# A four-token layout for the first 512 tokens, and a new split of the first loads over two DMA queues

## The chip, the cores and the metric

One core of one Trainium2 chip. The metric is the device time of one execution in microseconds, the median of several; the "span" of a profile is a little shorter (95.0 us in a run of 96.57). Runs are marked fast or slow; for one core, slow means over 1.5% above the fastest of the same kernel.

## The reference, cut to what matters

An mLSTM cell (4 batches, 8 heads, 768 tokens, head size 40) and behind it a maxout MLP.

```python
for t in range(S):
    m_new  = np.maximum(f_gate[:, :, t] + m, i_gate[:, :, t])
    f_stab = np.exp(f_gate[:, :, t] + m - m_new); i_stab = np.exp(i_gate[:, :, t] - m_new); m = m_new
    C = f_stab * C + i_stab * outer(v_t, k_t);  n = f_stab * n + i_stab * k_t      # shapes left out
    y[:, :, t] = sigmoid(o_gate_t) * (C @ q_t) / max(|n . q_t|, 1)
x = y.transpose(0, 2, 1, 3).reshape(B * S, H * D)      # 3072 x 320
out = maximum(x @ w1, x @ w2) @ w_out                  # 320 -> 1024 -> 320
```

The kernel uses that, with these gates, only the first 42 tokens add to the state to working accuracy. It checks this at run time and has a general path for other data, which never runs here.

## The kernel before: the parts that the change touches

SP, A, V, G are the queues or engines of SyncE, ScalarE, VectorE and GpSimd. `load_seg(g, ...)` loads tokens of batch 0: with `c1-c0` chunks, partition p holds that many neighbouring tokens, so one contiguous run is 160 bytes per chunk.

```python
SEG = ((0, 1), (1, 4), (4, 6))            # chunks of 128 tokens of batch 0 that are loaded together
...
SP.dma_start(out=f_sb[:, 0:L], in_=fv[:, 0:L])        # small: 16 KB
A.dma_start(out=i_sb[:, 0:L], in_=iv[:, 0:L])         # small: 16 KB
load_kv(0, 1, k, kst, SP)                             # small: 336 runs of 160 bytes
load_kv(0, 1, v, vst, A)
load_seg(0, q, qst, "qst", SP)                        # 1024 runs of 160 bytes
load_seg(0, o_gate, ost, "ost", A)
load_seg(1, q, qst, "qst", SP)                        # 1024 runs of 480 bytes
load_seg(1, o_gate, ost, "ost", SP)
load_w(0, 0, SP)                                      # then the weights, wo, later pieces: all SP
...
def idle(n):                                          # dummy matmuls, 512 columns each
    ...
idle(8)
# gates: F = cumsum(f); a = i - F; running maximum; Exp; transposed to gT   (V, A, TensorE)
# vw = v * gT on V; kT, vb (values), cq (the state) from TensorE through V
...
def f_h(n, pool=None, eng=V, dup=V):                  # chunk c of batch b
    first = c == 0                                    # first chunk: masked scores P; others: the state
    for s in range(NS):
        lhsT, rhs = (Pm[b][m, s, :], vb[b][m]) if first else (qT[b][rows(s), c, s, :], cq[b][rows(s)])
        nc.tensor.matmul(ph[...], lhsT, rhs[...], start=True, stop=True)
    ...                                               # y = (gate + 1) * ph          on V
    if n % 2:
        cp(dup)(out=y[:, DM:DM + 64], in_=y[:, 2 * DM:2 * DM + 64])    # a 64-column duplicate
...
f_h(1, pp_o, V, A); f_h(2, None); f_h(3, pp_o, V, A)  # duplicates on ScalarE
idle(3)
w_diff(0, 0, G); w_diffx(G); w_cast(0, 0, A)          # w1 - w2, and bf16 of w2
f_y(0, A, pp_o); idle(3); f_y(2, V)                   # transposes of y
g = up(0, 0, True)                                    # first MLP matmuls
...
```

`PLAN`, a table of two dozen lines, says which small operation of the later batches is issued beside which group of MLP matmuls.

## Time and profile before

| | before |
|---|---|
| median time | 96.83 us (96.66 to 97.06) |
| first MLP matmul | 13.54 us |
| from there to the last matmul's start | 78.1 us |
| from there to the end | 3.3 us |

After the first MLP matmul, TensorE has hardly a gap; so the time is the start of that stretch plus its length plus the tail.

### The profile page before, as it was taken

Reading aid. Unit: us, or ns where it says so; the run is one execution under the profiler, and the core shown is the slowest. Engines: PE = TensorE matmul, PEld = TensorE weight load, DVE = VectorE, ACT = ScalarE, POOL = GpSimd, SP = SyncE. Lnnn points to the kernel's source line nnn. Section 1 sums busy time; section 2 is a strip of 40 time slices with the busy share of each in tenths; the row PEclk is TensorE's granted clock in tenths of the full one; section 3 lists DMA queues with packets and bytes.
Section 4 is the critical chain, followed back from the end, with each engine's and each line's share of the span. In section 5 each row is a group of like instructions: output and inputs, shape, how many; then the busy total and the mean of one; then the engine's idle time right before and its main releaser. Section 6 shows DMA issues by size and latency. Waiting matters only on the chain.

```text
span 95.0 us, 2293 instructions
## 1 busy us (share of the span) xinstructions
PE 88.6 (93%) x884; PEld 65.3 (69%) x885; DVE 57.3 (60%) x167; ACT 42.0 (44%) x59; POOL 27.9 (29%) x67
## 2 busy tenths in 40 slices
PE   2998969999999999999999999999999999999960
PEld 1345547777788878688777868777686767877650
DVE  4997836953778999988843438649640442123240
ACT  0895784683241771391809068070713425070000
POOL 5146398763747070912271000002500000000000
PEclk9999999999999999999999999999999999999999
DMA  0999999997999989998969978393532030303052
GB/s 14 171 270 331 387 388 372 355 256 124 284 294 269 175 207 368 312 166 155 310 160 268 178 194 214 138 76 69 177 99 72 7 138 10 138 0 133 24 200 65
DMA packets 32701, 17.97 MB, mean 189 GB/s; under 512 B 21808, under 2 KB 30448, under 8 KB 32688
## 3 DMA queue, kind: packets, MB, share of 16 engines
q1 hardware_dynamic: 31250, 17.57, 71.9%
q10 hardware_dynamic: 1438, 0.23, 1.5%
q8 instruction: 7, 0.11, 0.5%
q14 instruction: 6, 0.05, 0.2%
HBM read 12.42 MB, written 3.93 MB: 172 GB/s over the span
## 4 chain that ended last, share of the span: by engine, by line
PE 79%; DMA 6%; DVE 6%; ACT 3%; SPq 1%; issue 1%; POOL 1%; POOLq 0%
PE po L548 28%; PE pu L479 17%; PE po L544 8%; PE pu L487 6%; DMA qst<-in_q_dram 6%; PE pwc L439 3%; PE pu L453 3%; PE ph L357 3%; PE pq L298 2%; PE py L389 2%; PE po L532 2%; DVE y L367 1%; DVE gt L493 1%; PE pu L460 1%; DVE qT L299 1%
## 5 line engine op out<-in xcount | busy, mean ns | idle before, releaser
L495 ACT ACTIVATE gt<-pu 128x1024 bf16<-128x1024 f32 x18 | 17.6, 1021 | 25.7 <-PE pu L487 24.6
L548 PE MATMUL po<-wo,gt 128*128 128x320 bf16 x160 | 26.9, 299 | 0.0
L479 PE MATMUL pu<-xT,wd 128*128 128x256 bf16 x160 | 20.9, 272 | 0.8 <-ACT xT L390 0.8
L556 DVE COPY o_sb<-po 128x320 f32<-128x320 f32 (+2 forms) x23 | 10.9, 474 | 17.2 <-PE po L548 17.2
L548 PEld LDWEIGHTS <-gt 128*128 128x128 bf16 x160 | 15.0, 98 | 5.2
L479 PEld LDWEIGHTS <-wd 128*128 128x128 bf16 x160 | 15.1, 97 | 3.9 <-issue 1.5
L367 DVE SCALAR_TENSOR_TENSOR y<-ost,ph 128x320 bf16<-128x320 f32 x20 | 9.6, 482 | 3.3 <-PE ph L357 2.2
L544 PE MATMUL po<-Wc_t,xT 128*128 128x320 bf16 (+2 forms) x50 | 10.7, 295 | 0.0
L267 ACT ACTIVATE ost<-ost 128x320 f32<-128x320 f32 (+2 forms) x14 | 8.7, 659 | 3.8 <-DMA ost<-in_o_gate_dram 3.8
L222 PE MATMUL pd<-warm,ident_b 128*128 128x512 bf16 x24 | 7.9, 449 | 1.7 <-POOL ident_b masks.py:199 1.7
L257 POOL CAST qb<-qst 128x240 bf16<-128x240 f32 (+1 forms) x12 | 5.8, 487 | 11.3 <-DMA qst<-in_q_dram 11.3
L487 PE MATMUL pu<-xT,wd 64*128 64x256 bf16 x80 | 6.1, 272 | 0.0
L576 POOL TENSOR_TENSOR a<-i_sb,F 32x640 f32<-32x640 f32 x1 | 1.5, 1528 | 15.5 <-DVE F L574 15.5
L402 POOL TENSOR_TENSOR wd<-w 128x512 bf16<-128x512 f32 x4 | 5.1, 1270 | 2.4 <-DMA w<-in_moe_w_dram 2.3
L544 PEld LDWEIGHTS <-xT 128*128 128x128 bf16 x50 | 4.0, 98 | 2.6 <-issue 1.5
L357 PE MATMUL ph<-cq,qT 120*128 120x123 bf16 (+1 forms) x60 | 5.7, 213 | 0.0
L548 PE MATMUL po<-wo,gs 128*128 128x320 bf16 (+2 forms) x40 | 5.6, 272 | 0.0
L463 ACT ACTIVATE gs<-pu 128x1024 bf16<-128x1024 f32 x4 | 3.9, 1016 | 3.4 <-PE pu L460 3.4
L357 PEld LDWEIGHTS <-qT 120*128 120x128 bf16 (+1 forms) x60 | 4.2, 98 | 1.5 <-ACT qT L299 0.4
L390 DVE COPY xT<-py 128x640 bf16<-128x640 bf16 x7 | 3.4, 492 | 2.7 <-PE py L389 2.5
L222 PEld LDWEIGHTS <-ident_b 128*128 128x128 bf16 x25 | 2.3, 111 | 3.7 <-issue 1.7
L298 PE MATMUL pq<-ident_b,qb 128*128 128x128 bf16 x48 | 4.1, 219 | 0.7 <-POOL qb L262 0.6
(131 smaller groups left out, 124.9 us busy)
## 6 DMA issues: line engine op xcount, KB each, us to landing
qst<-in_q_dram SPq DMA_DIRECT2D x3, 800.0 KB, 5.5
ost<-in_o_gate_dram SPq DMA_DIRECT2D x3, 800.0 KB
out_dram<-o_sb SPq DMA_DIRECT2D x7, 320.0 KB
w<-in_moe_w_dram SPq DMA_DIRECT2D x8, 256.0 KB, 5.4
out_dram<-o_sb SPq DMA_DIRECT2D x9, 160.0 KB, 2.3
wo_st<-in_moe_w_out_dram SPq DMA_DIRECT2D x2, 640.0 KB
qst<-in_q_dram SPq DMA_DIRECT2D x4, 160.0 KB
wx<-in_moe_w_dram SPq DMA_DIRECT2D x2, 256.0 KB
```

The source lines that it names most:

```text
L222: nc.tensor.matmul(pd[:, 0, :], ident_b, warm, start=True, stop=True)
L257: cp(eng)(out=qp[b % 2][:, c0:c1, 0:2, 0:HS3 * D].rearrange("p c s (h d) -> p c s h d", d=D), in_=qst[b][:, 0:6, c0:c1, :].rearrange("p (s ...
L267: A.activation(out=s, in_=s, func=AF.Tanh, scale=0.5)
L298: nc.tensor.transpose(pq[:, j, s, :], qb[b % 2][:, c0:c0 + 128], ident_b)
L357: nc.tensor.matmul(ph[:, vcols(s), :].rearrange("p a b -> p (a b)"), lhsT, rhs[:, vcols(s), :].rearrange("p a b -> p (a b)"), start=True, ...
L367: V.scalar_tensor_tensor(out=yo, in0=ost[b][:, :, c, :], scalar=1.0, in1=ph[:, :, 0:D], op0=OP.add, op1=OP.mult)
L479: nc.tensor.matmul(pus[i][:, j, :], wd[:, c, f * 128:(f + 1) * 128], x[:, :, GA[i][c], :], start=start and j % 2 == 0, stop=stop and j % 2 ...
L487: nc.tensor.matmul(pus[i][:, j, :], wd2[r, f * 128:(f + 1) * 128], x[r, :, 2, :], start=False, stop=stop and j % 2 == 1)
L495: A.activation(out=o, in_=pus[i], func=AF.Relu)
L544: nc.tensor.matmul(po, x[:, s // 2, GA[s % 2][cc], :], Wc_t[:, cc, w], start=False, stop=False)
L548: nc.tensor.matmul(po, gt[:, f, s % 2, s // 2 * L:(s // 2 + 1) * L], wo[:, f, w], start=False, stop=(f == NFF - 1))
L556: cp(eng)(out=o_sb[:, s % 2 if two else 0, :], in_=po)
```

## The change

The intent: hold tokens 4p to 4p+3 in partition p, so that q and o of the first 512 tokens come in 640-byte runs, half as many; start q's load at once by giving it the head of the SyncE queue; and shift weight work and two y transposes out of TensorE's full stretch.

```diff
-    SEG = ((0, 1), (1, 4), (4, 6))
+    SEG = ((0, 4), (4, 6))
+    TC = 11
@@ loads
-    SP.dma_start(out=f_sb[:, 0:L], in_=fv[:, 0:L])
+    load_seg(0, q, qst, "qst", SP)
+    A.dma_start(out=f_sb[:, 0:L], in_=fv[:, 0:L])
     A.dma_start(out=i_sb[:, 0:L], in_=iv[:, 0:L])
-    load_kv(0, 1, k, kst, SP)
+    load_kv(0, 1, k, kst, A)
     load_kv(0, 1, v, vst, A)
-    load_seg(0, q, qst, "qst", SP)
-    load_seg(0, o_gate, ost, "ost", A)
-    load_seg(1, q, qst, "qst", SP)
-    load_seg(1, o_gate, ost, "ost", SP)
+    load_seg(0, o_gate, ost, "ost", SP)
@@ all four chunks take the state; 11 rows of each are then overwritten (cut)
-        first = c == 0
+        first = b > 0 and c == 0
+        if n < 4:
+            yield
+            for s in range(NS):
+                nc.tensor.matmul(ph[0:TC, vcols(s), :]..., Pm[0][m, s, c, :], vb[0][m, vcols(s), :]..., ...)
@@ the mask with the gates in it: three fp32 products (six matmuls in the trace) and one V operation (cut)
+    for s in range(NS):
+        nc.tensor.matmul(pgi[0:KP, s], F[:, L + s * KP:L + s * KP + KP], gr, start=True, stop=True)
+    V.scalar_tensor_tensor(out=mask0[0:KP], in0=tcol0..., scalar=jrow[0:KP], in1=pgi[0:KP], ...)
@@ order (cut)
-    f_h(1, pp_o, V, A)
+    parts = [h_parts(n, (pp_o, pp_f, pp_f, pp_o)[n]) for n in range(4)]     # duplicates now on V
-    f_y(0, A, pp_o)
-    idle(3)
-    f_y(2, V)
+    idle(5)
+    f_y(0, A, pp_u)
+    run(w_trans(0, 0, A, pp_u))
+    f_y(2, V, pp_o)
+    w_fold(0, V, None)
@@ PLAN: every line rewritten; y transposes of pairs 6 and 8 by DMA instead of on TensorE
```

In front of the first MLP matmul stand 18 dummy matmuls instead of 25.

More of the change, by code (lines that the diff above doesn't have):

```diff
@@ L141 @@
     load_wo(1, SP)
-    load_seg(2, q, qst, "qst", SP)
-    load_seg(2, o_gate, ost, "ost", SP)
+    load_seg(1, q, qst, "qst", SP)
+    load_seg(1, o_gate, ost, "ost", SP)
     def load_batch(b, eng):
@@ L179 @@
     tcol = const.tile([128, L], BF, name="tcol")
+    tcol0 = const.tile([128, 4, TC], BF, name="tcol0")
+    ab = const.tile([128, B * NT, H], FP, name="ab")
+    mask0 = ab.rearrange("p n h -> p (n h)")[:, 0:NS * 4 * TC].rearrange("p (s c t) -> p s c t", c=4, t=TC)
     ge = const.tile([128, 2], FP, name="ge")
@@ L195 @@
     V.memset(vw[:, 0], 0.0)
+    G.tensor_copy(out=F[:, L:L + NS * KP].rearrange("p (h j) -> p h j", j=T0),
+                  in_=ident_f[:, 0:H9].unsqueeze(2).to_broadcast([BH, H9, T0]))
     G.memset(sel, 0.0)
     G.memset(vst[:, :, D:D1], 1.0)
-    for c in (1, 4):
+    for c in (4,):
         G.memset(qb[0][:, c * DM:c * DM + 64], 0.0)
+    G.iota(tcol0, pattern=[[1, 4], [4, TC]], base=0, channel_multiplier=0, allow_small_or_imprecise_dtypes=True)
     G.iota(tcol, pattern=[[1, L]], base=0, channel_multiplier=0, allow_small_or_imprecise_dtypes=True)
@@ L234 @@
                   in_=a[:, 0:T0].unsqueeze(1).to_broadcast([BH, HS3, T0]))
+    gr = F[:, L + NS * KP:L + NS * KP + 4 * TC].rearrange("p (c t) -> p c t", c=4)
+    A.activation(out=gr, in_=M[:, 0:4 * TC].rearrange("p (t c) -> p c t", c=4), func=AF.Exp, bias=mst, scale=-1.0)
     A.activation(out=aM, in_=aM, func=AF.Exp, bias=nmst, scale=1.0)
@@ L337, in f_s @@
     def f_s(b, pool=None):
+        if b == 0:
+            ps = ptile([128, NS, 4, TC], FP, "ps", pool)
+            for s in range(NS):
+                r = rows(s)
+                nc.tensor.matmul(ps[0:KP, s], kT[b][r, s].rearrange("p a b -> p (a b)"), qT[b][r, 0:4, s, 0:TC],
+                                 start=True, stop=True)
+            Pm[b] = ewp.tile([128, NS, 4, TC], BF, name="P0", tag="P", bufs=2)
+            V.tensor_tensor(out=Pm[b][0:KP], in0=ps[0:KP], in1=mask0[0:KP], op=OP.mult)
+            return
         ps = ptile([128, NS, 128], FP, "ps", pool)
@@ L348, in vcols, with f_h, h_parts @@
         return slice(HS3 * s, HS3 * s + NH[s])
-    def f_h(n, pool=None, eng=V, dup=V):
+    def f_h(*args):
+        run(h_parts(*args))
+    def h_parts(n, pool=None, eng=V, dup=V):
         b, c = bc(n)
-        first = c == 0
+        first = b > 0 and c == 0
         ph = ptile([128, H, D1], FP, "ph", pool)
@@ L358, in f_h @@
                              rhs[:, vcols(s), :].rearrange("p a b -> p (a b)"), start=True, stop=True)
+        if n < 4:
+            yield
+            for s in range(NS):
+                m = slice(0, NH[s] * T0)
+                nc.tensor.matmul(ph[0:TC, vcols(s), :].rearrange("p a b -> p (a b)"), Pm[0][m, s, c, :],
+                                 vb[0][m, vcols(s), :].rearrange("p a b -> p (a b)"), start=True, stop=True)
         if n // 2 not in ys:
@@ L370, in f_h @@
             cp(dup)(out=y[:, DM:DM + 64], in_=y[:, 2 * DM:2 * DM + 64])
+        if n < 4:
+            yield
         cp(eng)(out=nqb[:, n, :], in_=ph[:, :, D])
@@ L387, in f_y @@
         py = ptile([128, 5, 128], BF, "py", pool)
-        for i in range(5):
+        for i in (0, 1, 3, 4, 2):
             nc.tensor.transpose(py[:, i, :], y[:, i * 128:i * 128 + 128], ident_b)
@@ L430, in w_trans @@
             nc.tensor.transpose(pw[:, j, :], w2b[:, c, f * 128:f * 128 + 128], ident_b)
+        yield
         cp(eng)(out=w2T[:, c, half * 4:half * 4 + 4], in_=pw)
@@ L475, in up, with full @@
         pus = [pp_u.tile([128, 4, 2 * L], FP, name="pu", tag="pu") for _ in range(2)]
-        def full(i, c, j, start, stop):
+        def full(i, c, j, start, stop, p0=0, p1=2):
             f = half * 4 + j
-            nc.tensor.matmul(pus[i][:, j, :], wd[:, c, f * 128:(f + 1) * 128], x[:, :, GA[i][c], :],
-                             start=start and j % 2 == 0, stop=stop and j % 2 == 1)
+            nc.tensor.matmul(pus[i][:, j, p0 * L:p1 * L], wd[:, c, f * 128:(f + 1) * 128], x[:, p0:p1, GA[i][c], :],
+                             start=start and j % 2 == 0 and p0 == 0, stop=stop and j % 2 == 1)
         def rows64(stop):
@@ L577, in check_gates @@
         G.memset(bnd, 0.5)
-        G.tensor_scalar(out=bnd.rearrange("p (b c) h -> p b c h", c=NT)[:, :, 0, :],
-                        in0=gT[:, 1, :].rearrange("p (b h) -> p b h", b=B), scalar1=0.5, scalar2=None, op0=OP.mult)
+        G.tensor_scalar(out=bnd.rearrange("p (b c) h -> p b c h", c=NT)[:, 1:B, 0, :],
+                        in0=gT[:, 1, H:BH].rearrange("p (b h) -> p b h", b=B - 1), scalar1=0.5, scalar2=None, op0=OP.mult)
     def check_viol():
@@ L587, in check_viol @@
         V.tensor_tensor(out=ok_b[0:BH, 0:1], in0=viol[:, 1:2], in1=viol[:, 2:3], op=OP.mult)
-    ab = const.tile([128, B * NT, H], FP, name="ab")
     def check_abs():
@@ L611 @@
     V.scalar_tensor_tensor(out=jrow, in0=jrow, scalar=-float(T0), in1=prow, op0=OP.mult, op1=OP.add)
-    V.tensor_scalar(out=mask, in0=tcol, scalar1=jrow, scalar2=None, op0=OP.is_ge)
-    A.copy(out=kb[:, 1:B].rearrange("p b h d -> p b (h d)"),
-           in_=warm[:, 0:H9 * D].unsqueeze(1).to_broadcast([128, B - 1, H9 * D]))
-    A.copy(out=vw[:, 1:B].rearrange("p b h d -> p b (h d)"),
-           in_=warm[:, 0:H9 * D1].unsqueeze(1).to_broadcast([128, B - 1, H9 * D1]))
-    f_k(0, pp_o)
-    idle(2)
-    pg = pp_f.tile([128, 2, BH], FP, name="pg", tag="pf")
-    for j in range(2):
-        nc.tensor.transpose(pg[:, j, :], aM[:, j * L:(j + 1) * L], ident_f)
-    cast_q(0, 0, 1, G)
-    V.tensor_copy(out=gT, in_=pg)
-    prep_v(0, V)
     G.memset(fold, 0.0)
@@ L628 @@
                         pattern=[[0, 2], [-2, 64]], channel_multiplier=1)
-    idle(2)
-    f_q(0, A, 1)
-    V.reciprocal(out=gI, in_=gT[:, 1])
-    sigm(0, 0, 1)
-    idle(2)
-    f_v(0, pp_o)
-    f_s(0)
-    f_c(0, pp_o)
-    cast_q(0, 1, 3, G)
-    cast_q(0, 3, 4, A)
+    A.copy(out=kb[:, 1:B].rearrange("p b h d -> p b (h d)"),
+           in_=warm[:, 0:H9 * D].unsqueeze(1).to_broadcast([128, B - 1, H9 * D]))
+    pg = pp_f.tile([128, 2, BH], FP, name="pg", tag="pf")
+    for j in range(2):
+        nc.tensor.transpose(pg[:, j, :], aM[:, j * L:(j + 1) * L], ident_f)
+    V.tensor_copy(out=gT, in_=pg)
+    prep_v(0, V)
+    f_k(0, pp_o)
+    idle(3)
+    f_v(0, pp_o)
+    f_c(0, pp_o)
+    idle(2)
+    cast_q(0, 2, 4, A)
+    cast_q(0, 0, 2, G)
     G.memset(qb[0][:, QW:QW + 64], 0.0)
     pad_q(1)
-    idle(2)
-    f_q(1, A, 2)
-    sig_first(0, V)
-    f_h(0, pp_o)
-    f_q(3, V, 1)
-    sigm(0, 1, 2)
-    sigm(0, 2, 4)
-    idle(3)
-    f_h(1, pp_o, V, A)
-    f_h(2, None)
-    f_h(3, pp_o, V, A)
-    idle(3)
+    f_q(2, A, 2)
+    f_q(0, V, 2)
+    pgi = pp_o.tile([128, NS, 4, TC], FP, name="pgi", tag="po")
+    for s in range(NS):
+        nc.tensor.matmul(pgi[0:KP, s], F[:, L + s * KP:L + s * KP + KP], gr, start=True, stop=True)
+    V.scalar_tensor_tensor(out=mask0[0:KP], in0=tcol0[0:KP].unsqueeze(1).to_broadcast([KP, NS, 4, TC]),
+                           scalar=jrow[0:KP], in1=pgi[0:KP], op0=OP.is_ge, op1=OP.mult)
+    sigm(0, 0, 2)
+    sigm(0, 2, 4)
+    f_s(0, pp_u)
+    parts = [h_parts(n, (pp_o, pp_f, pp_f, pp_o)[n]) for n in range(4)]
+    for g in parts:
+        next(g)
+    next(parts[0])
+    next(parts[1])
+    run(parts[0])
+    next(parts[2])
+    next(parts[3])
+    for g in parts:
+        run(g)
     w_diff(0, 0, G)
@@ L655 @@
     w_cast(0, 0, A)
-    f_y(0, A, pp_o)
-    idle(3)
-    f_y(2, V)
+    idle(5)
[3 more added lines that the diff above has]
+    w_fold(0, V, None)
     w_castx(A)
+    w_diff(0, 1, G)
+    w_cast(0, 1, A)
     g = up(0, 0, True)
     next(g)
-    w_fold(0, V, pp_o)
-    w_fold(1, V, pp_o)
     next(g)
-    w_trans(0, 0, V)
-    w_diff(0, 1, G)
-    w_cast(0, 1, A)
+    w_transx(A, A)
     w_diff(1, 0, G)
-    w_cast(1, 0, A)
     w_diff(1, 1, G)
@@ L672 @@
     run(g)
-    w_cast(1, 1, A)
-    w_transx(V, A)
-    w_trans(0, 1, A, pp_o)
-    w_trans(1, 0, V)
+    w_cast(1, 0, A)
+    w_fold(1, V, None)
+    run(w_trans(0, 1, V, pp_o))
     g = up(0, 1, True)
     next(g)
+    run(w_trans(1, 0, V))
     next(g)
-    w_trans(1, 1, V, pp_o)
+    w_cast(1, 1, A)
+    run(w_trans(1, 1, A, pp_o))
+    V.reciprocal(out=gI, in_=gT[:, 1])
+    V.tensor_scalar(out=mask, in0=tcol, scalar1=jrow, scalar2=None, op0=OP.is_ge)
     next(g)
+    A.copy(out=vw[:, 1:B].rearrange("p b h d -> p b (h d)"),
+           in_=warm[:, 0:H9 * D1].unsqueeze(1).to_broadcast([128, B - 1, H9 * D1]))
     run(g)
@@ L710 @@
     PLAN = """
-v1 S1.0.1|S1.2.4 p2 q6 q8|S1.1.2 s1 q10 l2.4|S1.4.6 F1 p3 h6|S2.0.1 C2.0.1 h7|h8 l2.5
-l3.2 y6|h9||y8 h10||K2 V2 C2.1.3 C2.5.6
-l3.1 C2.3.5|k2 C3.0.1 h11|x14 l3.0|v2|c2|F2 S2.1.3 y10 q12
-q16 K3|s2|
-h13 S2.3.6|l3.3 l3.4 h12|V3|h16|y12|h14 h15 X14
-C3.1.3|h17|
-l3.5 x18|||C3.5.6|k3|C3.3.5
-x20|y16||||S3.0.1 F3
-|g0|x22|c3 v3||
-S3.1.3||s3|S3.3.6 h19|h18|
-|h20|h21 X20|||
-X18|h23||g1 h22||
-X22|||||g2
-||||g3|
+q6 v1 S1.0.1 S1.4.6 S1.1.2 l2.4 l2.5 l3.1||F1 s1 q10 S1.2.4|h6|q8 h7|h8
+y6|h9|h10|y8|K2 S2.1.3 l3.2|h11 V2
+k2|p2 S2.0.1|C2.0.1 C2.3.5|C2.1.3|C2.5.6 c2 q12|v2 s2
+l3.0 F2 p3 q16|h13 S2.3.6|
+x14 h12|l3.4 h16|K3 h15 C3.1.3||h14|X12 C3.0.1 V3
+X14|y10|C3.3.5 k3
+h17 x18||||l3.3 C3.5.6|l3.5
+|X16|x20|x22 S3.0.1||S3.1.3
+S3.3.6||F3 c3|||
+s3|g0|v3|h19|h18|X18
+|||h21 h20|g1|X20
+|h23|h22|X22||
 |||||
-|||||g4
-|||||g5
+g3|||||
 |||||
+|g2|g4|||
+|||||
+|||g5||
 |||||
@@ L881 @@
             nc.vector.tensor_copy(out=xg, in_=px)
-            gg = gtp.tile([128, NFF, L], BF, name="g_g", tag="gt")
-            for f in range(NFF):
-                pu = pp_u.tile([128, L], FP, name="g_pu", tag="pu")
-                for cc in range(2):
-                    nc.tensor.matmul(pu, wd[:, cc, f * 128:(f + 1) * 128], xg[:, cc, :],
-                                     start=(cc == 0), stop=False)
-                nc.tensor.matmul(pu, wd2[0:64, f * 128:(f + 1) * 128], xg[0:64, 2, :], start=False, stop=True)
-                nc.scalar.activation(out=gg[:, f, :], in_=pu, func=AF.Relu)
+            pu = pp_u.tile([128, DFF], FP, name="g_pu", tag="pu")
+            for h in range(0, DFF, 512):
+                for cc in range(2):
+                    nc.tensor.matmul(pu[:, h:h + 512], xg[:, cc, :], wd[:, cc, h:h + 512], start=(cc == 0), stop=False)
+                nc.tensor.matmul(pu[:, h:h + 512], xg[0:64, 2, :], wd2[0:64, h:h + 512], start=False, stop=True)
+            gu = gtp.tile([128, DFF], BF, name="g_gu", tag="gt")
+            nc.scalar.activation(out=gu, in_=pu, func=AF.Relu)
+            pt = pp_f.tile([128, NFF, L], BF, name="g_pgt", tag="pf")
+            for f in range(NFF):
+                nc.tensor.transpose(pt[:, f, :], gu[:, f * L:(f + 1) * L], ident_b)
+            gg = gtp.tile([128, NFF, L], BF, name="g_g", tag="gt")
+            nc.scalar.copy(out=gg, in_=pt)
             po = pp_o.tile([128, DM], FP, name="g_po", tag="po")
```

## The prediction

> **What bounds the kernel now.** I read the page from the top: busy shares, the forty slices, the chain of waits; then the time line of the first 14 us engine by engine, the busy time by stretch, and TensorE's own time line. Busy shares and stretches of the kernel before:
>
> ```profile
> PE 88.6 (93%) x884; PEld 65.3 (69%) x885; DVE 57.3 (60%) x167; ACT 42.0 (44%) x59; POOL 27.9 (29%) x67
> ...
> 0.00:13.54 13.54, 10.48 (x70) 5.28 (x72) 10.39 (x44) 8.73 (x16) 6.57 (x24) 1.00 0.91 253
> 13.54:20.25 6.71, 6.66 (x71) 5.09 (x71) 4.18 (x7) 4.45 (x8) 5.11 (x5) 1.00 1.09 350
> 20.25:92.00 71.75, 71.44 (x746) 54.96 (x743) 42.55 (x116) 28.79 (x37) 16.20 (x39) 1.00 0.69 166
> ```
>
> The columns of the stretches are its length, then busy time and count of TensorE, weight loads, VectorE, ScalarE and GpSimd, the granted clock, the DMA share and GB/s. From 13.54 us on, TensorE is busy 78.1 of 78.5 us: no other engine can be the bound there, and only less TensorE work, or fewer of its stalls, shortens it. Before 13.54 us, TensorE's 10.5 us are mostly dummy matmuls (25 of 512 columns) that keep it warm; what counts there is when the first real matmul of the MLP can start. The chain of waits says what it waits for:
>
> ```profile
> 2.46 5.40 DMA qst<-in_q_dram
> 8.00 0.73 POOL qb L262
> 8.77 0.52 PE pq L298 x6
> 9.31 0.80 ACT qT L299
> 12.38 0.52 ACT w2b L405
> 12.90 0.60 ACT xT L390
> 13.54 0.60 PE pu L479 x4
> ```
>
> Start, length, what. The second piece of q (chunks 1 to 3, 480-byte runs) lands just before 8.00; casts, transposes and copies lead to the gated outputs y, their transposes xT, and the first MLP matmul at 13.54. VectorE's time line shows the last part of that chain:
>
> ```profile
> 11.14 0.49 DVE L367 SCALAR_TENSOR_TENSOR y<-ost,ph 128x320 bf16<-128x320 f32 x1
> 11.55 0.16 DVE L371 COPY nqb<-ph 128x8 f32<-128x8 f32 x1
> 11.62 0.48 DVE L367 SCALAR_TENSOR_TENSOR y<-ost,ph 128x320 bf16<-128x320 f32 x1
> 12.02 0.16 DVE L371 COPY nqb<-ph 128x8 f32<-128x8 f32 x1
> 12.81 0.49 DVE L390 COPY xT<-py 128x640 bf16<-128x640 bf16 x1 [0.64 <-PE py L389]
> ```
>
> The fourth y ends at 12.10; xT of both pairs exists at 13.3 to 13.5. The tail after the last matmul (91.6 us) is copies and the last store, 3.3 us.
>
> **What the Trainium skill says.** (1) "DMA: Bandwidth & Descriptors", Specifications, puts the smallest transfer at line rate at 512 bytes. The trace agrees: counted from its packet records, 480-byte packets went at 310 per half us (298 GB/s), 2048-byte ones at 95 (389 GB/s); a median packet takes 14 ns at 160 bytes, 31 at 480, 27 at 512, 88 at 2048. (2) The same page, "Issuing engines are not separate DMA queues": queues interleave on the same 16 engines, so moving gates, k and v to the ScalarE queue buys only issue order and issue time. (3) "TensorE: Matmul & The Clock Gate", "Back-to-back issue gap": an isolated warm matmul needs N/2.4 + 2.5 ns, 56 ns at 128 columns and 216 at 512; the trace's dummies and transposes are spaced just so (216 and 56 to 57 ns). (4) "ScalarE: Activation LUTs", "What ACT_TABLE_LOAD costs": about 1283 ns; the trace has 2.62 to 3.90. It comes after ScalarE's DMA issues, so a fourth issue delays it.
>
> **The change part by part.** In the new layout token 4p+c sits in partition p of chunk c for all of the first 512 tokens, so the first 42 tokens are 11 partitions of each of four chunks. All four chunks take the state path, and 12 small matmuls overwrite 11 rows.
>
> *DMA.* q's first 655 KB become 1024 packets of 640 bytes instead of 1024 of 160 and 1024 of 480; o the same. Estimate for 640 bytes, from 27 ns at 512 and 88 at 2048: 32 ns. Ahead of q's end lie 64 gate packets, 672 of k and v, 1024 of q: (64x27 + 672x14 + 1024x32)/16 = 2.75 us, from the first packet at 2.08 to 4.8. Before, q's second piece wrote its last semaphores at 7.2 and was cast at 8.00; with the same 0.8 us lag q is usable at about 5.7. The output gate adds 2.05 us (7.7). The first weights pair lands about 9.1; before, GpSimd started on it at 10.98.
>
> *Gate path.* The fourth ScalarE issue (0.4 us) moves the table load to end near 4.3; tiny, the new small Exp and the 0.51 us Exp end near 5.2 (4.75 before). k, now third, lands about 0.45 us later, near 4.5; the small VectorE operations after it (0.74 us before) end near 5.5. Then in sequence, by before's durations: gT 0.2, vw 0.73, kT 0.55, vb 0.5, cq 0.54, most starting as the previous one ends: cq ends near 7.9 (8.96 before).
>
> *q path.* ScalarE's cast waits for its 1.07 us copy and ends near 6.9. TensorE, in program order behind pv, pc and two dummies, transposes 12 blocks from 7.4 to 8.1 (12x57 ns); VectorE copies half of them 8.2 to 8.8. Scores, masked product (132 columns instead of 384, about 0.25), 12 state matmuls (0.62) and the first overlays put the first y near 10.0. Four y at 0.48 and two small copies end near 12.0, transposes and xT copy near 12.9. **First MLP matmul 12.9 instead of 13.54: -0.6.** The q data comes 2.3 us sooner but only this much arrives, because vw, kT, vb, cq, qT, mask, product and four y now stand in one VectorE row.
>
> *TensorE work after that point.* Counting instructions in both programs: one weight transpose group (4x57 = 0.23) and one fold (0.22) move ahead of the first MLP matmul, into time in which TensorE waits anyway: -0.44. Two of eight y transpose groups (5x57 = 0.28 each) become DMA transposes: -0.56. All other matmuls after 13.54 have the same counts and columns.
>
> *Stalls.* TensorE's spacing shows true waits of 0.17 + 0.21 us where both halves of the first unit hand over their PSUM, which stay (the hand-over is paced by a relu of 1.0 to 1.24 us), and 0.25 at 29.7 and 0.22 at 38.3 us, behind VectorE copies. The rewritten plan spreads q6, q8, q10 and k2, c2 apart, so I count half of these: -0.2. Tail: 0.
>
> Sum: -0.6 - 0.44 - 0.56 - 0.2 = -1.8; I take -1.75, as more things can be late than early: 96.83 - 1.75 = **95.1 us** (-1.8%).
>
> **Rivals.** *The start is VectorE-bound and gains nothing.* For: the row above; 12 extra overlays, a larger qT copy, late k. Then first matmul at 13.5, time 95.7. *The start follows the DMA.* If the latencies overlap better than I count, it starts near 12.2, 94.4. For: q 2.3 us and weights 1.9 us sooner. Against: the four y alone need 1.9 us after their inputs. *TensorE cools down.* Dummies before the first MLP matmul fall from 25 to 18, with waits near 8.2 to 8.9. Before's first seven ran at 426 ns spacing, half speed; cold transposes would cost some 0.5 us: 95.6. Against: no wait as long as before's first 2 us. *A new wait later.* Two more DMA transposes (2.7 us from issue to landing) lie where the DMA share is high; a late xT would stall TensorE and give back 0.5: 95.6. *GpSimd becomes the pace* with four 1.27 us weight differences plus one: 9.1 + 5x1.28 = 15.5, before the second half's last need near 17.8; not a bound.
>
> **Range and chances.** The start is uncertain by 0.5 either way, the stalls and DMA transposes by 0.4, run-to-run by 0.2: 94.0 to 96.3. The 2% line lies at 94.9, just below my number: faster 0.43, within 2% 0.54, slower 0.03. Slower by 2% needs a start 1 us later and all savings lost.
>
> **What would show it.** First pu matmul at 12.9 (12.3 to 13.4); casts of q near 5.8; VectorE without gaps from about 5.5 to 9; first weight difference near 9.2; six y groups on TensorE; 78.1 us from first to last matmul falling to about 76.9; the waits at 29.7 and 38.3 gone or not. I would be wrong if the aM Exp comes far after 5.2, if k's cast on VectorE waits beyond 5, if weights gate the first matmul, or if new TensorE gaps over 0.3 us appear after 13 us.

## More of the kernel before

VectorE's time line: the columns are start, length, engine, line, operation, tiles and forms, count; a wait stands in brackets at the end where the engine sat idle before.

```profile
3.12 0.28 DVE L228 TENSOR_TENSOR a<-i_sb,F 32x128 f32<-32x128 f32 x1
...
4.20 0.32 DVE L240 CAST kb<-kst 42x320 bf16<-42x320 f32 x1
...
6.16 0.72 DVE L243 TENSOR_TENSOR vw<-vst,gT 42x328 bf16<-42x328 f32 x1
```

The i gate is used at 3.12, k at 4.20, v at 6.16, and no line has a bracket: none of the three loads is waited for.

## The result, and the profile after

The changed kernel takes **105.53 us** (median of 4; 105.46, 105.59 and 104.90 fast, 108.09 slow). The ratio is 1.0876, with an interval of 1.0821 to 1.0931: 8.8% slower. Ratios here are the mean time of one kernel's fast runs over that of the other's in the same rounds, so not quite the ratio of the medians quoted.

First, by stretch; columns as in the prediction's table of stretches.

```profile
0.00:22.28 22.28, 15.84 (x86) 9.51 (x88) 11.89 (x45) 7.59 (x12) 13.58 (x31) 1.00 1.00 288
22.28:28.68 6.40, 6.16 (x66) 4.71 (x66) 3.36 (x7) 5.61 (x10) 0.27 (x1) 1.00 1.16 294
28.68:101.00 72.32, 71.23 (x736) 54.32 (x733) 41.49 (x114) 29.21 (x38) 13.81 (x36) 1.00 0.56 135
```

The first MLP matmul starts at 22.28 instead of 13.54. From it to the last matmul's start it is 78.2 us, against 78.1. So the whole loss, 8.7 us, lies before the first MLP matmul. The chain of waits leads there (start, length, what):

```profile
2.68 7.22 DMA vst<-in_v_dram
...
10.03 1.47 DVE vw L250
...
11.54 0.43 PE pv L338
...
12.00 0.47 PE pc L329 x3
12.47 0.85 PE pd L227 x2
13.32 1.28 PE pq L305 x12
14.60 1.43 PE pgi L662 x6
16.04 0.44 PE ps L349 x3
16.48 1.10 PE ph L376 x12
17.58 1.20 PE ph L382 x12
```

The first piece is not q but v, 54 KB, issued at 2.68 and used at 10.03. VectorE's time line shows all three small loads waited for:

```profile
5.43 0.28 DVE L233 TENSOR_TENSOR a<-i_sb,F 32x128 f32<-32x128 f32 x1 [1.97 <-DMA i_sb<-in_i_gate_dram]
...
7.74 0.32 DVE L247 CAST kb<-kst 42x320 bf16<-42x320 f32 x1 [0.77 <-DMA kst<-in_k_dram]
...
10.03 1.46 DVE L250 TENSOR_TENSOR vw<-vst,gT 42x328 bf16<-42x328 f32 x1 [1.18 <-DMA vst<-in_v_dram]
```

i is used 2.3 us later than before, k 3.5, v 3.9. q itself came as forecast: GpSimd casts it at 5.61. The trace's packet records give the landings, as the last semaphore writes of each transfer: i 4.78 and q 4.89; k 6.91 and o 7.22; v 9.12. Before, f and i had landed by 2.4 and k by 4.0. The small transfers land in step with the big ones of the other queue. (k and v have 14 such writes in every run here, the others 16.)

The second thing to see is in TensorE's part of the chain: 12 transposes (pq) take 1.28 us, 107 ns each, where the same transposes need 56 to 57 ns in the kernel before; the two dummies take 427 ns each, not 216. TensorE works at half speed from its first matmul to 20.7 us: there the spacing of its matmuls falls from 427 ns (dummies) to 56 ns (transposes), and there, at 20.67, lies the first clock record in the trace. The granted clock in the table of stretches is 1.00 all the same: here that column reads 1.00 before the first record. A loss after the first record it does show: in e7 below, a table of stretches gives 0.50 from 9.3 to 12.6 us.

### The profile page after: what moved, and what is told of

It reads as the page before. It is cut to its first block, busy times and chain, and to the rows that moved or that the text cites. A ratio compares the mean times of both kernels' runs of the same rounds, so it can differ in the third digit from the quotient of the medians.

```text
span 103.9 us, 2292 instructions
## 1 busy us (share of the span) xinstructions
PE 93.2 (90%) x885; PEld 68.5 (66%) x886; DVE 56.8 (55%) x165; ACT 42.4 (41%) x58; POOL 27.7 (27%) x67
## 3 DMA queue, kind: packets, MB, share of 16 engines
HBM read 12.42 MB, written 3.93 MB: 157 GB/s over the span
## 4 chain that ended last, share of the span: by engine, by line
PE 61%; DMA 18%; ACT 4%; SPq 4%; POOL 3%; DVE 3%; ACTq 1%; issue 1%; DVEq 0%; POOLq 0%
PE po L576 19%; PE pu L507 10%; DMA vst<-in_v_dram 7%; DMA qst<-in_q_dram 6%; DMA ost<-in_o_gate_dram 5%; PE po L572 5%; PE pu L481 3%; SPq L294 3%; PE pwc L467 3%; PE ph L376 3%; PE pu L515 3%; PE pd L227 3%; PE pq L305 3%; ACT gt L523 2%; POOL qb L264 2%; ACT ost L274 2%
## 5 line engine op out<-in xcount | busy, mean ns | idle before, releaser
L507 PE MATMUL pu<-xT,wd 128*128 128x256 bf16 x160 | 20.3, 273 | 1.2 <-ACT gt L523 0.8
L274 ACT ACTIVATE ost<-ost 128x640 f32<-128x640 f32 (+2 forms) x13 | 8.4, 691 | 7.8 <-DMA ost<-in_o_gate_dram 5.7
L376 PE MATMUL ph<-cq,qT 120*128 120x123 bf16 (+1 forms) x63 | 6.3, 228 | 0.2 <-DVE nqb L398 0.2
L376 PEld LDWEIGHTS <-qT 120*128 120x128 bf16 (+1 forms) x63 | 4.9, 108 | 1.8 <-issue 0.4
L306 DVE COPY qT<-pq 128x768 bf16<-128x768 bf16 x7 | 3.9, 553 | 2.0 <-PE pq L305 2.0
```

The lines of the kernel that those rows point to most:

```text
L274: A.activation(out=s, in_=s, func=AF.Tanh, scale=0.5)
L376: nc.tensor.matmul(ph[:, vcols(s), :].rearrange("p a b -> p (a b)"), lhsT, rhs[:, vcols(s), :].rearrange("p a b -> p (a b)"), start=True, ...
L507: nc.tensor.matmul(pus[i][:, j, p0 * L:p1 * L], wd[:, c, f * 128:(f + 1) * 128], x[:, p0:p1, GA[i][c], :], start=start and j % 2 == 0 and ...
```

## The experiments

Theory A: the small transfers are delayed behind the large one on the other queue, and the long wait leaves TensorE at half speed. Rival B: the new layout, with its longer row on VectorE and TensorE, costs the time. "First matmul" is the first MLP matmul in the profile.

| run | i used | k used | v used | first matmul | median us (fast runs) |
|---|---|---|---|---|---|
| before | 3.12 | 4.20 | 6.16 | 13.54 | 96.8 |
| changed | 5.43 | 7.74 | 10.03 | 22.28 | 105.5 (104.9 to 105.6) |
| e1 old queues | 3.40 | 4.51 | 6.07 | 14.72 | 97.1 |
| e2 queue move in the old layout | 4.15 | 6.44 | 8.88 | 16.56 | (98.9, 99.4) |
| e3 q and o in four pieces | 3.93 | 6.13 | 7.33 | 16.29 | 99.8 (99.2 to 100.1) |
| e4 21 more dummies | 5.54 | 7.88 | 10.01 | 19.40 | 102.9 |
| e8 f ahead of q | 3.40 | 4.70 | 6.99 | 15.12 | 98.6 (98.1 to 98.8) |
| e12 queues exchanged | 5.31 | 7.75 | 8.96 | 19.29 | 101.5 (100.4 to 100.5) |

The profile of e12 is of a slow run: its columns i, k, v and first matmul go with that run, not with the fast times beside them.

**e1_old_queues: only the queues undone.**

```diff
-    load_seg(0, q, qst, "qst", SP)
-    A.dma_start(out=f_sb[:, 0:L], in_=fv[:, 0:L])
+    SP.dma_start(out=f_sb[:, 0:L], in_=fv[:, 0:L])
     A.dma_start(out=i_sb[:, 0:L], in_=iv[:, 0:L])
-    load_kv(0, 1, k, kst, A)
+    load_kv(0, 1, k, kst, SP)
     load_kv(0, 1, v, vst, A)
+    load_seg(0, q, qst, "qst", SP)
```

> The changed kernel with the first six DMA issues back in the old order (f, k, then q and o on the SyncE queue; i and v on the ScalarE queue); all else as changed. Theory A (the small loads starve behind q on the other queue, and the long wait leaves TensorE at half speed): v lands before 5.5 us instead of 9.9, the first MLP matmul starts at 12.5 to 14 instead of 22.3, time 95 to 97.5 us. Rival B (the four-token layout and its longer VectorE and TensorE row cost the time): the first MLP matmul stays after 17 us, time over 100 us.

Measured: 97.08 us, ratio to before 0.9997 (0.9943 to 1.0051). Six lines of issue order account for 8.4 us (105.5 to 97.1) of the 8.7 (105.5 to 96.8). Theory A holds, B falls as the main cause, though the first matmul, at 14.72, is 0.7 us later than theory A allowed. But this run also shows that the rest of the change, free of the queues, is worth nothing: 97.1, not the 95.1 that was predicted. VectorE and GpSimd in it:

```profile
11.20 1.26 POOL L435 TENSOR_TENSOR wdx<-wx 128x512 bf16<-128x512 f32 x1
11.56 0.93 DVE L395 COPY y<-y 128x64 bf16<-128x64 bf16 x1
...
12.49 0.87 DVE L392 SCALAR_TENSOR_TENSOR y<-ost,ph 128x320 bf16<-128x320 f32 x2
12.55 2.64 POOL L429 TENSOR_TENSOR wd<-w 128x512 bf16<-128x512 f32 x2
...
13.39 0.46 DVE L395 COPY y<-y 128x64 bf16<-128x64 bf16 x1
```

A copy of 64 columns takes 0.93 us on VectorE and ends (12.49) just after GpSimd's weight difference ends (12.46); the third and fourth y wait behind it. This is taken up in e5.

**e2_before_new_queues: the queue move alone, in the old layout.** The old kernel with q's first two pieces and o's on SP, and f, i, k, v on A.

```diff
+    load_seg(0, q, qst, "qst", SP)
-    SP.dma_start(out=f_sb[:, 0:L], in_=fv[:, 0:L])
+    A.dma_start(out=f_sb[:, 0:L], in_=fv[:, 0:L])
     A.dma_start(out=i_sb[:, 0:L], in_=iv[:, 0:L])
-    load_kv(0, 1, k, kst, SP)
+    load_kv(0, 1, k, kst, A)
     load_kv(0, 1, v, vst, A)
-    load_seg(0, q, qst, "qst", SP)
-    load_seg(0, o_gate, ost, "ost", A)
     load_seg(1, q, qst, "qst", SP)
+    load_seg(0, o_gate, ost, "ost", SP)
```

> The kernel before with the queue move alone: q's first two pieces and o on the SyncE queue, gates, k and v on the ScalarE queue; old layout. Theory A: i, k and v land late again (k and v after 6 us), the first MLP matmul moves from 13.5 to 16 to 21, time 99 to 105 us. Rival B: within 1 us of the kernel before, 96 to 98 us.

Measured: two fast runs of 98.89 and 99.38 and two slow ones (101.1); the fast ones are some 2.4 us over the kernel before. The move hurts without the new layout, at the low end of what was expected. The landings repeat the pattern: q's first piece 3.29 and i 3.71; q's second 5.77 and k 5.45; o 6.78 and v 6.50. f, the first on ScalarE's queue, got through at once (2.5); after it, each small transfer comes with the next large one of the other queue. q's first piece is only 160 KB here, so i loses less.

**e3_split_q: q and o in four transfers each.**

```diff
-    load_seg(0, q, qst, "qst", SP)
+    for h0 in range(0, H, 2):
+        load_part(q, qst, "qst", SP, h0, h0 + 2)      # two heads: 16 runs per DMA engine, not 64
...                                                     # o the same
```

> The changed kernel with q's and o's first pieces each cut into four DMAs of two heads (256 runs of 640 bytes, 16 per DMA engine, instead of 1024, 64 per engine) on the same queue in the same order. If the DMA engines alternate between the queues whole transfer by whole transfer, i is let in after a quarter of q: it lands near 3.2 instead of 4.8, k near 4, v near 5, and time falls to 97 to 100 us. If the queues share by packets, or i is late for its own issue, the landings and the time (105.5) stay within 1 us.

Measured: 99.78 us, ratio 1.029. i landed at 3.3, k at about 5.4, v at 6.1 instead of 4.8, 6.9 and 9.1. The same bytes in the same order on the same queues, only cut, bring back 5.7 of the 8.7 us (105.5 to 99.8). k and v came 1.1 to 1.4 us later than I had said. Still, what the small ones wait for is shown to be the large uncut transfer and not their own issue: ScalarE issued them at the same times.

**e4_warm: dummies so that TensorE stays busy.** `idle(8)` became `idle(20)`, `idle(3)` became `idle(12)`.

> The changed kernel with 21 more dummy matmuls (20 instead of 8 at the start, 12 instead of 3 behind the k transposes), so that TensorE is busy until vw is ready; loads untouched. If half speed of TensorE between 8 and 20.7 us is a real part of the loss, the first MLP matmul comes 2 to 3.5 us sooner (18.8 to 20.3) and the time is 102 to 103.5 us. If the wait for v alone is the loss, the time stays within 0.7 us of 105.5.

Measured: 102.85 us, ratio 1.0645; first matmul 19.40. The loads are as late as before (v used at 10.01), yet 2.9 us of the start come back. TensorE's time line of this run:

```profile
11.95 0.30 PE L338 MATMUL pv<-vw,sel 128*126 128x328 bf16 x1
12.09 0.33 PE L329 MATMUL pc<-vw,kb 128*120 128x123 bf16 x3
...
12.69 0.83 PE L305 MATMUL pq<-ident_b,qb 128*128 128x128 bf16 x12
13.45 0.85 PE L662 MATMUL pgi<-F 32*126 32x44 f32 x6
14.23 0.35 PE L349 MATMUL ps<-qT,kT 120*126 120x44 bf16 x3
14.43 0.77 PE L376 MATMUL ph<-cq,qT 120*128 120x123 bf16 x12
```

pq took 0.83 us here and 1.48 in the same view of the changed kernel, pgi 0.85 and 1.50. vw took 0.49 us here and 1.46 there, where it ran beside GpSimd's weight difference, but that gained nothing here: pv, which needs vw, stood behind the added dummies and began at 11.95, later than in the changed kernel (11.54). From the pc matmuls (12.00 there, 12.09 here) to the first MLP matmul it is 10.3 us there and 7.3 here. So half speed costs about 3 us of the 8.7, an estimate from these two stretches. Together with e1 the loss of the start roughly adds up: against e1, v is used 4.0 us later, vw takes 1.0 longer and half speed costs 3.0, in sum 8.0; e1 lost about 1.0 of its own in the two copies shown there. The measured difference is 7.6 (14.72 to 22.28).

**e8_gates_first: only f back ahead of q.** i, k, v are then first to third on A.

```diff
+    SP.dma_start(out=f_sb[:, 0:L], in_=fv[:, 0:L])
     load_seg(0, q, qst, "qst", SP)
-    A.dma_start(out=f_sb[:, 0:L], in_=fv[:, 0:L])
```

> The changed kernel with only the f gate put back ahead of q on the SyncE queue, so that i, k and v are first, second and third on the ScalarE queue. If a small transfer on the ScalarE queue gets in only at the boundaries of SyncE's large transfers, i (issued with f, before q) is on time near 2.4, k lands with q near 5 to 5.5, v with o near 7; the first MLP matmul is at 16 to 18.5, time 99 to 101.5. If only the gates' lateness mattered, the time falls to 97.

Measured: 98.56 us, ratio 1.0182; first matmul 15.12, better than expected. i is on time. k, issued at 1.50, a moment before q at 1.52, landed at 4.3, ahead of q (5.8), where I had expected it with q. v, issued at 2.20, landed at 6.1 and VectorE waited 1.0 us for it. So being further back in the row of transfers costs here too: about 1.5 us against e1, where k and v were each second on a queue; v is the only one of the three that VectorE waited for.

**e12_swapped: the queues exchanged.** q, then o on A; f, i, k, v, then the weights on SP.

> The changed kernel with the two queues' parts exchanged: q, then o on the ScalarE queue; f, i, k, v, then the weights on the SyncE queue. If the engines take the two queues in turn, transfer by transfer, whichever queue is which, i still lands with q near 4.8, k with o near 7, v after it, and the time is 103.5 to 106.5. If the SyncE queue is simply served first, f, i, k and v land before 4 us and the time is 96.5 to 98.

Measured: fast runs 100.4 to 100.5, ratio 1.0381. i landed at 4.7 with q (5.0), k at 6.9 with o (7.4), v after it at 7.5: the same picture with the queues exchanged, so it isn't that one queue is served first. The time is 3 us below what I expected. In the profile, v was used 1.1 us sooner than in the changed kernel and clear of the weight difference. That profile is of a slow run, and its clock records show TensorE at full speed from 5.8 to 9.2 us, at half speed again until 12.6 (its q transposes are 107 ns apart), at full speed until 19.5 and once more at half until 22.9. Its granted clock is 0.967, two such stretches of 3.4 us in 102.7; the three fast runs list 0.983, which would fit one (an estimate: half of 3.4 us in 99). Why the speed was lost is not shown.

The "Queues, rings and completion order" section of the Trainium skill's "DMA: Bandwidth & Descriptors" says that an engine takes turns between queues packet by packet, a packet holding at most 64 descriptors. q has 1024/16 = 64 runs per engine, so i waiting for all of q fits that ceiling, and so does i getting in after a quarter in e3. The 9 to 17 descriptors that the section calls typical don't fit: the first of i's packets moved at 4.2 us, some 2 us after the first of q's, where 17 runs of 32 ns would be 0.5 us (an estimate). Turns by whole transfer would fit as well; no run here was made to tell the two apart.

**Mending the rest.** Four runs go from e1 towards what the prediction had promised of the layout.

**e5_dup_act: the duplicate copies on ScalarE**, as they were before the change.

```diff
-    parts = [h_parts(n, (pp_o, pp_f, pp_f, pp_o)[n]) for n in range(4)]
+    parts = [h_parts(n, (pp_o, pp_f, pp_f, pp_o)[n], V, A) for n in range(4)]
```

> The old-order kernel of the first experiment with the two 64-column duplicate copies of y moved from VectorE to ScalarE. In that run the first took 0.93 us and the second 0.46 us on VectorE, both ending as a weight difference on GpSimd ended. If these copies wait for GpSimd and for nothing else, the four y follow each other within 1.7 us, the first MLP matmul starts 0.8 to 1.3 us sooner (13.4 to 13.9 instead of 14.7), time 95.8 to 96.4. If the y chain waits for something else, it stays at 14.4 or later and the time at 97.

Measured: 97.02 us, ratio 1.001, first matmul 14.39.

```profile
10.53 0.89 DVE L392 SCALAR_TENSOR_TENSOR y<-ost,ph 128x320 bf16<-128x320 f32 x2 [0.47 <-PE ph L382]
11.40 0.87 DVE L392 SCALAR_TENSOR_TENSOR y<-ost,ph 128x320 bf16<-128x320 f32 x2
...
12.31 0.24 ACT L395 COPY y<-y 128x64 bf16<-128x64 bf16 x1 [0.62 <-DVE y L392]
12.46 0.61 ACT L432 CAST w2b<-w 128x512 bf16<-128x512 f32 x1
```

The four y now follow each other and end at 12.3 instead of 13.4: the copies had waited for GpSimd. "SBUF — State Buffer" of the skill, section "SBUF: two separate sides", has VectorE and GpSimd share one port pair, which GpSimd and certain VectorE operations hold as a lock for a whole instruction; this pair of runs agrees, with 0.93 against 0.18 us for a copy that ran free in the changed kernel. But the start moved by 0.3 only: ScalarE does the copies ahead of the first weight cast, TensorE waits for that cast, and y's second transposes stand behind it. A new wait took the place of the old one.

**e6_fewer_idle: and four dummies less** (`idle(2)` ahead of q's transposes gone, `idle(5)` to `idle(3)`).

> As the run with the copies on ScalarE, and two dummies less ahead of q's transposes and two less ahead of y's. If dummies stand in the way of ready work: transposes of q at 7.3 instead of 7.7, first MLP matmul another 0.2 to 0.5 us sooner. If TensorE then loses its full speed, later.

Measured: 96.67 us, ratio 0.9991, first matmul 14.07: 0.3 sooner, as said, and TensorE kept full speed.

**e7_mask_early: and the mask's fp32 matmuls before q's transposes, in place of three dummies.**

```diff
-    idle(3)
+    pgi = pp_u.tile([128, NS, 4, TC], FP, name="pgi", tag="pu")
+    ...                                                  # the matmuls and the V operation, moved up
     f_v(0, pp_o)
```

> As the run with fewer dummies, and the mask's 6 fp32 matmuls with their VectorE product moved from behind q's transposes to behind the k transposes, in place of three dummies. They cost 0.85 us of TensorE and 0.35 us of VectorE in the y chain: if that chain sets the start, the first y comes near 10.0 instead of 10.6, the first MLP matmul at 12.4 to 13.0, time 94.8 to 95.8 us, below the kernel before. If vb or cq is delayed by it instead, no gain over the run with fewer dummies.

Measured: fast runs 96.9 to 97.8 (four of eight were slow), ratio 1.0015, first matmul 15.19: a miss. In the profiled run (97.76) TensorE did the 12 state matmuls in 1.27 us instead of 0.77: half speed again, from 9.25 to 12.66 us by the clock records, after 3.4 us in which it was busy for 2.5. It had three dummies less than e6, and q landed 0.5 us later in this run; which of the two lost the speed is not shown (e11 lacks the same three, has one more at the start, and keeps it).

**e9_cast_first: e6, with the first weight cast ahead of the copies on ScalarE.**

```diff
+    w_cast(0, 0, A)
     parts = [h_parts(n, (pp_o, pp_f, pp_f, pp_o)[n], V, A) for n in range(4)]
...
-    w_cast(0, 0, A)
```

> As the run with fewer dummies, and the first weight cast put ahead of the duplicate copies in ScalarE's program. In that run ScalarE did the copies (11.1 to 12.2), then the cast (12.1 to 12.75), for which the first weight transposes on TensorE waited 1.2 us, with y's second transposes behind them. If that order is what holds the start, the first MLP matmul comes at 12.9 to 13.4 instead of 14.07 and the time is 95.2 to 96.2, below the kernel before. If not, 96.7 as it was.

Measured: first matmul 13.19, as expected; time 96.48 us, ratio 0.9979 (0.9936 to 1.0023), above the range. The start is now 0.35 ahead of the kernel before, yet the time is not clearly better: from the first matmul to the last it takes 77.98 us.

**e10_old_plan: e9 with the old plan of the later batches** (and so two more y transposes on TensorE, two fewer by DMA).

> The same with the old plan of the steady part (what is issued beside which matmul group, and with two more y transposes on TensorE, two less by DMA). If the new plan's two DMA transposes save their 0.56 us and its waits are fewer, this one is 0.5 to 1 us slower than the run it is made from. If the new plan's own waits (0.36 near 43 us, 0.17 near 47, 0.3 to 0.9 near 59) give the saving back, the two are within 0.4 us.

Measured: **95.90 us**, ratio 0.9908 (0.9876 to 0.9939): faster than e9 (neither of my two cases), and the only version below both kernels beyond doubt, though by less than 2%. The new plan does save its TensorE work: with every matmul from the first MLP matmul on counted at the commonest spacing of its kind, e9 has 0.56 us less than e10. But what the stretch takes beyond that count is 1.06 us more in e9. The chain of waits of e9 names the largest new wait:

```profile
31.05 5.26 DMA qst<-in_q_dram
...
36.37 0.59 POOL qb L264
...
38.04 5.01 DMA qT<-qb
...
43.09 0.32 PE ph L376 x3
```

A DMA transpose of q takes 5.0 us from issue, in a stretch of busy DMA, and TensorE stands 0.6 us before its 43.09. With the old plan the largest wait there is 0.25 us.

**e11_mask_early_warm: e9 with the early mask and one more dummy at the start.**

> The cast ahead of the copies, and the mask's matmuls early as in the run that tried this, with one more dummy at the start. If that run lost by half speed of TensorE alone, TensorE is at full speed by 7 us here and the first MLP matmul comes 0.3 to 0.6 us sooner than in the run with the cast first: time 94.8 to 95.8. If the early mask delays vb and cq, or TensorE is again at half speed at 9 to 12 us, it is slower than that run.

Measured: first matmul 13.00, 0.2 sooner than e9, full speed held in the profiled run (96.70); but ratio to before 1.0042 (0.9966 to 1.0117), fast runs 96.4 to 97.8, two of six slow, three of six with a granted clock of 0.982, and the stretch to the last matmul 78.8 us. Inconclusive as a version. For e7 it fits that half speed had cost the start, but the cast put first and q, 0.5 us sooner than in e7, have a part in the 2.2 us between the two.

## Why the prediction was wrong

Predicted 95.1 us (94.0 to 96.3, and a chance of 0.03 for a clear slowdown), measured 105.5.

- **DMA, q.** Right. 640-byte packets had a median of 32 ns; q was cast at 5.61 (said 5.7). The weights were used at 9.88 (said 9.1).
- **Gate path: the step that failed.** The prediction said that the queue move "buys only issue order and issue time" and that k "lands about 0.45 us later, near 4.5". k was cast at 7.74, the Exp of aM, put at 5.2, ended at 7.58 (the prediction had named both as signs of being wrong), and v, for which no delay was counted at all, was used at 10.03; vw had been put at about 5.7. Adding up bytes on shared engines had been right for q and wrong for what shares with q: i's 16 KB waited for q's 655 KB, k for o, v for the weights. e1 shows that the issue order as a whole is the cause, e3 that the size of the transfer ahead is, e12 that it isn't the queue's identity.
- **TensorE cools down.** Named as a rival, at 0.5 us; its size was about 3 (e4). I had argued from short waits in a start that was itself wrong.
- **q path, first matmul at 12.9.** With the old queues it came at 14.72. The prediction did not name the wait of the two copies for GpSimd, and left out the mask's matmuls, 0.85 us on TensorE at full speed. Of the 1.5 us down to 13.19 (e9), 0.3 came with the copies on ScalarE (e5), 0.3 with four dummies less (e6) and 0.9 with the weight cast ahead of the copies (e9).
- **TensorE work, -1.0 us.** Right: by the count at the commonest spacing, the work after the first MLP matmul fell by 1.0 us from the kernel before to the changed one (0.56 of it between e10 and e9); the first half-unit became 0.31 shorter (6.71 to 6.40), not 0.44.
- **Stalls, -0.2.** Wrong in sign: what the stretch takes beyond that count grew by 1.1 us (before to changed; the same for e10 to e9). New waits of the changed kernel are 0.36 us at 51.2 and 0.76 at 66.7.
- **Steady part and tail.** 78.1 to 78.2 us in sum: the gains and the new waits cancel.

## What to carry to other kernels

When a small load that everything waits for shares the DMA engines with a large one, ask which is issued first and how large the other's pieces are; in these runs a second queue did not let the small one past. Put small, early-needed loads at the head of both queues, or cut the large one. And when a start gets a longer wait, ask twice more: does TensorE lose its full speed in it, and does the later start put VectorE's copies beside GpSimd's work.

## What the Trainium skill lacked or had wrong

- "DMA: Bandwidth & Descriptors", "Issuing engines are not separate DMA queues": read alone it says that a second queue changes little. Here six lines of issue order moved the time by 8.4 us (105.5 to 97.1). The section on queues and completion order of the same page has the 64-descriptor ceiling, which fits, beside a typical 9 to 17, which doesn't; it gives no number for what a small transfer loses: 2.3 us for 16 KB behind 655 KB.
- "TensorE: Matmul & The Clock Gate", Part 1, gives about 3.4 us of sustained work for full speed. From 12.0 to 18.8 us of the changed kernel TensorE issued transposes and small matmuls nearly without a gap and stayed at half speed (107 ns per transpose); it rose at 20.7, in a row of dummies. The page's Part 4 says that transposes don't count as busy in the same way; that matmuls of 44 to 123 columns did not suffice either is not there. In e1 the same work kept a full speed that TensorE had reached before it (12 transposes in 0.83 us).
- The granted clock of the profile was 1.00 while TensorE ran at half speed before the first clock record (20.67 us); the spacing of equal matmuls (427 against 216 ns) shows it. No page says that of this view.
- "SBUF — State Buffer" has the lock between VectorE and GpSimd right, but gives no number for a short copy: 0.93 us instead of 0.18.
